# First MLP in blocks: six buffers for y on its way out, the next group's x fetched as soon as blocks are made, own banks for the last chunk's y, another lag count for VectorE

## The chip, the cores and the metric

One core of one Trainium2 chip. The metric is the device time of one execution in microseconds (us). Of the kernel before there are three timed runs, 1055.63, 1056.96 and 1057.51 us (median 1056.96), and one profiled execution of 1056.06 us whose span in the trace is 1054.2 us.

## The reference

Everything is float32. Attention with random features feeds a two-layer MLP, and that a gated one:

```python
def phi(x):                      # x scaled by D**-0.25, omega is 128 x 64
    h = x @ omega.T - (x * x).sum(-1, keepdims=True) / 2
    return exp(h - h.max(-1, keepdims=True)) / sqrt(128)
num, den = phi(q) @ (phi(k).T @ v), phi(q) @ phi(k).sum(seq) + 1e-6
x = (num / den) rearranged from (4, 8, 576, 64) to (2304, 512)
h = x @ w_in                                                  # 512 -> 2048
y = (maximum(h, 0) + alpha * minimum(h, 0)) @ w_out           # 2048 -> 512
out = ((y @ w_a) * (y @ w_b)) @ w_out2                        # 512 -> 1536 -> 512
```

## The kernel before

**Products.** Each float32 operand is split into a high part and a low part, and a product is three matmuls (high by high, high by low, low by high). ScalarE makes a high part by a copy (`xh`, `gh`, `w`), VectorE the low part by a subtraction (`xl`, `gl`, `w` again).

**Weights** lie in DRAM as raw bits. A decoder (`D_`) loads a raw tile, has ScalarE make `z` and `r` from it and VectorE run a chain `z`, `a`, a custom instruction on `a`, and the low half of `w`; some pieces are stored (`store`) and fetched again later (`w<-store`). `D_.pace()` runs the next decode steps as long as `behind()`, the modelled lag of VectorE behind TensorE, is small. That model is `dve_cost` (L181): per instruction a fixed 0.15 and so many columns per us. `hilo(q)` asks for weight q and first runs all the decoding that is still missing up to it, at once.

**Stages.** Times are of the span. To 264.8 us: attention, and beside it the first 4 of 16 feature blocks of the first MLP in 9 chunks of 256 rows (class `Mlp`: `front` makes h, prelu and the split, `back` multiplies by the output weights and sums y in PSUM; `yo` is y on its way to DRAM, `ypart`). From 264.8 to 599.9 us: the other 12 feature blocks in nine groups, n = 0 to 8, each a third of the features (`ps`) by a third of the rows (`tp`), in the order (0,0), (0,1), (0,2), (1,2), (1,1), (1,0), (2,0), (2,1), (2,2). From 599.9 us: the gated MLP in nine groups of the same kind.

**A group of the first MLP** has a `gate_dual` (L1183), seven products of block sums of x and of weights (`GATE_NAMES`: A11, A12, S1, S2, S4, S3, A22) for two halves m, and a `gate_back` (L1227), eight output tiles of 12 matmuls. A product leaves PSUM by ScalarE (`s_g`, `e_g`, `u_g`) or is added on VectorE. Products accumulate in banks named by chain, W, E and B. S2, S3 and A22 are each added onto what stands in the bank of chain W, so each starts only when ScalarE has copied out the one before (`s_g`, then `u_g` twice). An output tile leaves through `leave` (L1252): ScalarE copies it to `yp`, one of three buffers of the tag "op" in pool `io`, and GpSimd's queue sends it with an add to `ypart`.

**x of the next group.** If the next group has other rows, a generator `gens(n)` (L1270) loads them (`load_x`, tile `xg`, from `xpart`) at the group's start, lets one step pass and then runs `combine`, which forms the sums on VectorE (`sumS1g`, ...) and splits each block (`xhg..`, `xlg..`). `tick` takes one step of the generator at every second half-product; what is emitted is what stands in each engine's queue, in that order. Groups 0, 1, 3, 4, 6 and 7 are followed by other rows; group 8 prepares the gated MLP's first rows from `ypart`; groups 2 and 5 prepare nothing.

**The gated MLP.** Per group two `dual` calls (j = 0, 1) and a `back` (L1080), output `o`. The output weights of groups 0, 3 and 6 are decoded as they are first needed.

**Queues.** All loads, and the stores of weights, are issued in order from one queue, SP's (`load_dma`); `ypart<-yp` from GpSimd's (POOL).

Of the kernel before, what the change touches and what calls it, by code (L numbers as in the profile page):

```python
# [9 lines left out]
F32 = mybir.dt.float32  # L10
F32R = mybir.dt.float32r
U32 = mybir.dt.uint32
AF = mybir.ActivationFunctionType
# [5 lines left out]
P = 128  # L19
# [3 lines left out]
DM = 512  # L23
# [11 lines left out]
CI = 256  # L35
# [4 lines left out]
TN = 384  # L40
# [17 lines left out]
def tile_kernel(ctx: ExitStack, tc: tile.TileContext, qT, kT, v1, omT, wbits, alpha, out):  # L58
# [21 lines left out]
    def t_(pool, tag, name, cols=TN, dt=F32, bufs=None):  # L80
        return pool.tile([P, cols], dt, tag=tag, name=name, bufs=bufs)
# [73 lines left out]
        load["dve"] += 0.1 + cols_of(out) / 960  # L155
        vector.tensor_tensor(out=out, in0=in0, in1=in1, op=op)

    clock = {"pe": 0.0, "dve": 0.0, "dma": 0.0}

    def size_of(ap):  # L160
        return math.prod(ap.shape[1:])
# [19 lines left out]
    def dve_cost(name, *a, out=None, in_=None, **k):  # L181
        out = a[0] if out is None else out
        n = size_of(in_ if name == "tensor_reduce" else out)
        clock["dve"] = max(clock["dve"], clock["pe"]) + (0.15 + n / 1890 if name == "tensor_scalar" else 0.15 + n / 960)

    def load_dma(out, in_):
        n = size_of(out) * 4 * P if out.shape[0] == P else 0
# [265 lines left out]
    class Mlp:  # L453
# [7 lines left out]
        def tile(self, kind, name, dt=F32R):  # L461
            n = self.n[kind] = self.n.get(kind, -1) + 1
            m, i, c = n // 4 % 2, n // 2 % 2, n % 2
            if kind in ("xh", "xl"):
                return t_(gp, f"g{kind[1]}{m}{i}{c}", name, dt=dt)[:, :CI]
            if kind == "u":
                return t_(tpb, f"u3{c}", name, dt=dt)[:, :CI]
            return t_(tpa, ("s1" if kind == "gh" else "e5") + "001"[n % 3], name, dt=dt, bufs=(2, 2, 1)[n % 3])[:, :CI]

        def banks(self, psh, tag):  # L470
            self.psy = st_p.enter_context(tc.tile_pool(name="psy", bufs=2, space=PSUM))
# [16 lines left out]
        def front(self, o, n, f, last):  # L488
            hilo(2 * f + 1)
            passed(24 * n / 2400)  # L490
            load["act"] += n / 1000
            load["dve"] += 1.2 * n / 1000
            wh, wl = hilo(2 * f)
            hp = self.psh.tile([P, 512], F32, tag=self.htag, name=f"h{o}_{f}")[:, :n]
            parts = [[(wh, 0)], [(wl, 0)], [(wh, 1)]] if f == 0 else [[(wh, 0)], [(wh, 1)], [(wl, 0)]]
            i = 0
            for part in parts:
                for k in range(KT):
                    ks = slice(k * P, (k + 1) * P)
                    for w_, low in part:  # L500
                        tensor.matmul(hp, lhsT=w_[:, ks], rhs=self.xs[o, k][low],
                                      start=(i == 0), stop=(i == 3 * KT - 1))
                        i += 1
                if D_.free_run:
                    D_.pace(PACE, 1)
            D_.free[2 * f] = last
            u_ = self.tile("u", f"u{o}_{f}", F32)
            nc.scalar.activation(u_, hp, AF.Relu, scale=-1.0)
            vector.scalar_tensor_tensor(out=hp, in0=u_, scalar=bend[:, f:f + 1], in1=hp,
                                        op0=ALU.mult, op1=ALU.add)  # L510
            gh = self.tile("gh", f"gh{o}_{f}")
            gl = self.tile("gl", f"gl{o}_{f}")
            load["act"] += n / 1000
            load["dve"] += 1.3 * n / 1000

            def low():
                vector.tensor_tensor(out=gl, in0=hp, in1=gh.bitcast(F32), op=ALU.subtract)

            def high():
                nc.scalar.activation(gh, hp, AF.Copy)  # L520

            self.gs[o, f] = (gh, gl)
            self.beside(high, low)
            self.q.append((o, n, f, last))

        def back(self, o, n, f, end):
            first, last = f == 0, f == NF0 - 1
            if first:
                ts = [self.psy.tile([P, 2, 256], F32, tag="y", name=f"y{o}_{e}") for e in range(2)]
                self.ys[o] = [ts[e // 2][:, e % 2, :n] for e in range(KT)]  # L530
            ys = self.ys[o]
            wh, wl = hilo(2 * f + 1)
            gh, gl = self.gs.pop((o, f))
            for e in range(KT):
                es = slice(e * P, (e + 1) * P)
                for i, (w_, r_) in enumerate(((wh, gh), (wh, gl), (wl, gh))):
                    tensor.matmul(ys[e], lhsT=w_[:, es], rhs=r_,
                                  start=(first and i == 0 and e % 2 == 0), stop=(last and i == 2 and e % 2 == 1))
                if D_.free_run and e % 2:
                    D_.pace(PACE, 1)  # L540
            D_.free[2 * f + 1] = end
            if last:
                for e in range(KT):
                    if e % 2 == 0:
                        yo = io.tile([P, DM], F32, tag="op", name=f"yo{o}_{e}", bufs=3).rearrange("p (e n) -> p e n", e=2)
                        nc.scalar.activation(yo[:, 0], ys[e], AF.Copy)
                    else:
                        vector.tensor_copy(yo[:, 1], ys[e])
                        nc.sync.dma_start(out=ypart[:, e - 1:e + 1, o:o + n], in_=yo)
                self.ys.pop(o)  # L550

# [440 lines left out]
        return h[:, 256 * i:256 * i + 256], l[:, 256 * i:256 * i + 256]  # L992

    later = []

    def drain(n=1):
        for _ in range(n):
# [11 lines left out]
    def dual(ps, tp, j, last, gen=None, g0=0):  # L1009
        nm_ = f"{ps}{tp}{j}"  # L1010
        banks, sb = [{}, {}], [{}, {}]

        def keep(m, nm, bufs):
            sb[m][nm] = t_(tpb if nm in ("u3", "w7") else tpa, f"{nm}{m}", f"{nm}{m}_{nm_}", bufs=bufs)
            return sb[m][nm]

        for p, nm in enumerate(A_NAMES):
# [18 lines left out]
            E = [e if e is None else e[:, :TN] for e in E]  # L1036
            if nm == "A11":
                for m in range(2):
                    act(keep(m, "s1", 2 - m), W[m])
            elif nm == "S1":  # L1040
                for m in range(2):
                    act(keep(m, "e5", 2 - m), E[m])
            elif nm == "S2":
                for m in range(2):
                    act(keep(m, "u2", 2 - m), W[m])
            elif nm == "S4":
                for m in range(2):
                    vec(sb[m]["u2"], E[m], sb[m]["u2"], ALU.add)
                vec(sb[0]["u2"], sb[0]["u2"], sb[1]["u2"], ALU.mult)
            elif nm == "S3":  # L1050
                for m in range(2):
                    act(keep(m, "u3", 1), W[m])
                split(ps, tp, j, 0, 1, sb[0]["u2"])()
            elif nm == "A12":
                for m in range(2):
                    vec(sb[m]["s1"], banks[m]["B"][:, :TN], sb[m]["s1"], ALU.add)
                vec(sb[0]["s1"], sb[0]["s1"], sb[1]["s1"], ALU.mult)
                if j:
                    low = split(ps, tp, j, 0, 0, sb[0]["s1"])
                else:  # L1060
                    low = lambda: None
                    later.append(lambda: split(ps, tp, j, 0, 0, sb[0]["s1"])())
                for m in range(2):
                    vec(sb[m]["e5"], sb[m]["u3"], sb[m]["e5"], ALU.add)
                low()
            else:
                act(keep(0, "w7", 1), W[0])
                vec(sb[0]["w7"], sb[0]["w7"], W[1], ALU.mult)
                vec(sb[0]["e5"], sb[0]["e5"], sb[1]["e5"], ALU.mult)
                later.append(lambda: split(ps, tp, j, 1, 1, sb[0]["e5"])())  # L1070
                later.append(lambda: split(ps, tp, j, 1, 0, sb[0]["w7"])())
# [66 lines left out]
                    next(gen, None)  # L1138
                D_.pace(PACE, 1)

    agenda, now = [], [0]

    def soon(n, fn):
        agenda.append((now[0] + n, fn))
# [39 lines left out]
    def gate_dual(ps, tp, last, gen):  # L1184
# [1 line left out]
        banks, sb = [{}, {}], [{}, {}]  # L1186

        def keep(m, nm):
            sb[m][nm] = t_(tpb if nm == "u3" else tpa, f"{nm}{m}", f"{nm}{m}_g{ps}{tp}",
                           bufs=1 if nm == "u3" else 2 - m)  # L1190
            return sb[m][nm]

        for p, nm in enumerate(GATE_NAMES):
# [39 lines left out]
    def gate_back(ps, tp, last, gen):  # L1233
        q = Q0 + QA * ps + 7
        for i in range(2):
            for e in range(KT):
# [13 lines left out]

                def leave(ob=ob, e=e, i=i):
                    o = tp * 2 * TN + i * TN  # L1252
                    op = io.tile([P, DM], F32, tag="op", name=f"yp{ps}_{o}_{e}", bufs=3)[:, :TN]
                    act(op, ob)
                    nc.gpsimd.dma_start(out=ypart[:, e, o:o + TN], in_=op, accum_op=ALU.add)  # L1255

# [10 lines left out]
    last_of = lambda n: n % NTP == NTP - 1  # L1267
    follow = lambda n: seq[n + 1] if n + 1 < len(seq) and seq[n + 1][1] != seq[n][1] else None

    def gens(n):  # L1270
        if n == 0:
            yield from first_x
            yield
        if n + 1 == len(seq):
            load_x(ypart, 0)
            yield from combine(A_NAMES, "00")
        elif follow(n):
            load_x(xpart, follow(n)[1])
            yield
            yield from combine(GATE_NAMES, "g%d%d" % follow(n))  # L1280

    for n, (ps, tp) in enumerate(seq):
        gen = gens(n)
        gate_dual(ps, tp, last_of(n), gen)
        gate_back(ps, tp, last_of(n), gen)
        for _ in gen:
            pass
    tick()
    while agenda:
        tick()  # L1290
# [72 lines left out]
```

## Time and profile before

| | |
|---|---|
| timed runs, median (lowest to highest) | 1056.96 us (1055.63 to 1057.51) |
| profiled execution, its own time | 1056.06 us |
| its span in the trace | 1054.2 us |
| mean granted TensorE clock | 0.961 of full |
| TensorE (PE) busy | 960.1 us, 91% |
| VectorE (DVE) busy | 700.1 us, 66% |
| ScalarE (ACT) busy | 595.5 us, 56% |
| GpSimd (POOL) busy | 238.8 us, 23% |
| moved by DMA | 159.96 MB, 152 GB/s on average |

The engines run beside each other, each through its own queue in order. So TensorE's idle time, and the time it runs at a lower granted clock, is what a change to the other engines can give back; an engine's idle time that TensorE doesn't wait for costs nothing. Rows of the trace give start and length in us and, in square brackets, how long the engine was idle just before and what released it.

### The profile page before, as it was taken

Reading aid. Unit: us, or ns where it says so; the run is one execution under the profiler, and the core shown is the slowest. Engines: PE = TensorE matmul, PEld = TensorE weight load, DVE = VectorE, ACT = ScalarE, POOL = GpSimd, SP = SyncE. Lnnn points to the kernel's source line nnn. Section 1 sums busy time; section 2 is a strip of 40 time slices with the busy share of each in tenths; the row PEclk is TensorE's granted clock in tenths of the full one; section 3 lists DMA queues with packets and bytes.
Section 4 is the critical chain, followed back from the end, with each engine's and each line's share of the span. In section 5 each row is a group of like instructions: output and inputs, shape, how many; then the busy total and the mean of one; then the engine's idle time right before and its main releaser. Section 6 shows DMA issues by size and latency. Waiting matters only on the chain.

```text
span 1054.2 us, 17763 instructions
## 1 busy us (share of the span) xinstructions
PE 960.1 (91%) x6663; PEld 895.6 (85%) x6663; DVE 700.1 (66%) x1460; ACT 595.5 (56%) x1440; POOL 238.8 (23%) x226
## 2 busy tenths in 40 slices
PE   8999999987898979898978997999969999959998
PEld 7788898876898979898977995989968999949997
DVE  5887887965756546864595476677574866583633
ACT  6866777753555645665474555565555565544541
POOL 4666556670022102111201200000001010001000
PEclk9999999998899989999999998999989999989999
DMA  8634675567664885397616622335415278405232
GB/s 292 225 122 165 218 275 198 180 230 282 228 138 70 239 253 109 77 241 193 163 20 158 159 81 70 130 136 204 180 39 123 78 161 256 83 21 120 32 59 60
DMA packets 64853, 159.96 MB, mean 152 GB/s; under 512 B 6144, under 2 KB 28032, under 8 KB 64768
## 3 DMA queue, kind: packets, MB, share of 16 engines
q1 hardware_dynamic: 49504, 135.90, 36.7%
q0 software_dynamic: 15120, 22.81, 15.9%
q8 instruction: 52, 0.85, 0.3%
q14 instruction: 33, 0.27, 0.1%
q10 hardware_dynamic: 144, 0.13, 0.0%
HBM read 96.43 MB, written 62.39 MB: 151 GB/s over the span
## 4 chain that ended last, share of the span: by engine, by line
PE 56%; DVE 17%; ACT 11%; DMA 9%; issue 4%; POOL 2%; SPq 0%; ACTq 0%; DVEq 0%; POOLq 0%
PE o L173 13%; PE W L173 12%; PE y L173 11%; PE E L173 6%; DVE a L173 4%; DMA ypart<-yp 3%; DMA xg<-xpart 3%; ACT ph L655 3%; PE B L173 3%; PE W_g L173 3%; PE h L173 2%; DVE xl L483 2%; DVE u_g L173 1%; POOL ypart L1255 1%; DVE w L173 1%
## 5 line engine op out<-in xcount | busy, mean ns | idle before, releaser
L173 PE MATMUL o<-w,gh 128*128 128x512 f32 x432 | 141.1, 407 | 29.3 <-ACT w L148 28.6
L1255 POOL DMA_DIRECT2D ypart<-yp x72 | 63.0, 874 | 304.1 <-ACT yp L148 154.2
L173 PEld LDWEIGHTS o<-w,gh 128*128 128x128 f32 x432 | 84.4, 196 | 51.3 <-ACT w L148 30.9
L1119 POOL DMA_DIRECT2D out<-op x30 | 26.2, 872 | 405.1 <-ACT xh11S L148 195.7
L173 PE MATMUL o<-w,gl 128*128 128x512 f32 x216 | 86.6, 401 | 0.0
L148 ACT ACTIVATE yp<-y 128x384 f32<-128x384 f32 x72 | 35.2, 488 | 79.5 <-DMA ypart<-yp 54.7
L173 PE MATMUL y<-gh,w 128*128 128x256 f32 x288 | 61.9, 298 | 8.5 <-DVE yo L173 8.5
L148 ACT ACTIVATE op<-o 128x512 f32<-128x512 f32 x51 | 30.5, 598 | 59.0 <-PE o L173 43.9
L148 ACT ACTIVATE u<-W 128x384 f32<-128x384 f32 x72 | 35.0, 493 | 46.4 <-PE W L173 45.8
L173 DVE TENSOR_SCALAR z<-z 128x512 uint32<-128x512 uint32 x41 | 17.3, 423 | 60.0 <-ACT z L235 59.8
L173 PEld LDWEIGHTS y<-gh,w 128*128 128x128 f32 x288 | 49.0, 198 | 8.9 <-DVE yo L173 8.9
L173 DVE CUSTOM_DVE_ANT_0 a<-a,r 128x1024 uint16<-128x1024 uint16 x68 | 49.2, 723 | 5.9 <-ACT u L148 0.5
L173 PE MATMUL h<-xh,w 128*128 128x256 f32 x288 | 50.0, 300 | 3.2 <-ACT xh L480 1.3
L173 PEld LDWEIGHTS o<-w,gl 128*128 128x128 f32 x216 | 42.3, 196 | 8.8
L237 POOL TENSOR_SCALAR z<-raw 128x512 f32<-128x512 f32 x28 | 44.2, 1579 | 17.1 <-DMA raw<-in_w 17.0
L240 ACT ACTIVATE r<-raw 128x512 uint32<-128x512 uint32 x68 | 46.3, 683 | 0.8 <-DMA raw<-in_w 0.8
L173 PEld LDWEIGHTS h<-xh,w 128*128 128x128 f32 x288 | 40.6, 198 | 5.2 <-ACT xh L480 1.7
L244 POOL TENSOR_SCALAR a<-raw 128x512 f32<-128x512 f32 x27 | 42.5, 1575 | 0.0
L173 PE MATMUL y<-gl,w 128*128 128x256 f32 x144 | 41.8, 290 | 0.0
L173 DVE TENSOR_TENSOR w<-a,w 128x512 fp32r<-128x512 f32 (+1 forms) x27 | 17.0, 630 | 29.4 <-ACT w L148 29.4
L520 ACT ACTIVATE gh<-h 128x256 fp32r<-128x256 f32 x36 | 13.9, 385 | 38.8 <-DVE h L173 38.8
L173 DVE TENSOR_TENSOR u<-E,u 128x384 f32<-128x384 f32 x36 | 19.1, 553 | 20.5 <-PE E L173 18.8
(1270 smaller groups left out, 3128.9 us busy)
## 6 DMA issues: line engine op xcount, KB each, us to landing
raw<-in_w SPq DMA_DIRECT2D x68, 512.0 KB, 5.5
w<-store SPq DMA_DIRECT2D x47, 512.0 KB, 5.4
store<-t_None SPq DMA_DIRECT2D x41, 512.0 KB, 3.0
ypart<-yp POOLq DMA_DIRECT2D x72, 192.0 KB, 4.7
xg<-ypart SPq DMA_DIRECT2D x14, 768.0 KB, 7.0
xg<-xpart SPq DMA_DIRECT2D x12, 768.0 KB, 9.9
out<-op POOLq DMA_DIRECT2D x30, 256.0 KB, 5.0
q<-in_qT SPq DMA_DIRECT2D x8, 576.0 KB, 4.9
```

The lines of the kernel that those rows point to most:

```text
L148: nc.scalar.activation(out, in_, AF.Copy)
L173: return call(*a, **k)
L237: nc.gpsimd.tensor_scalar(out=z.bitcast(F32), in0=high, scalar1=2.0 ** -112, scalar2=None, op0=ALU.mult)
L240: nc.scalar.activation(r, self.raw[i][:, :, 0], AF.Copy, scale=2.0 ** -29)
L244: nc.gpsimd.tensor_scalar(out=sg.bitcast(F32), in0=high, scalar1=0.0, scalar2=None, op0=ALU.mult)
L483: nc.vector.tensor_tensor(out=lo, in0=src, in1=hi.bitcast(F32), op=ALU.subtract)
L520: nc.scalar.activation(gh, hp, AF.Copy)
L655: nc.scalar.activation(ph[:, 2 * pr + j], pair[j][:, o + pr], AF.Exp, bias=nm[:, j, o + pr:o + pr + 1])
L1119: nc.gpsimd.dma_start(out=dst, in_=op, accum_op=ALU.add)
L1255: nc.gpsimd.dma_start(out=ypart[:, e, o:o + TN], in_=op, accum_op=ALU.add)
```

## The change

- **Buffers.** The tiles that hold a product on its way (`s1`, `e5`, `u2`, and `gh`, `gl` of class `Mlp`) take nine named slots a0 to a8 of pool `tpa`. The groups of the first MLP use six of them, so `yp` alternates between the three buffers of "op" and the free slots a1, a4 and a7.
- **x.** `load_x` of the next other rows is issued as soon as `combine` has formed the blocks of the ones before. The list `todo` keeps what is next, and `combine` starts one step into a group (three in group 0, behind the rest of the x blocks begun in the last chunk).
- **Last chunk.** Its y lies in PSUM banks of the pool behind `bank()`, not in the two of `psy`. Neither `front` nor `back` runs `D_.pace` in it.
- **yo.** Once attention is over, ScalarE copies both halves of `yo`; before, VectorE copied the second.
- **Lag count.** `tensor_scalar` counts 0.12 less in the model. The fixed part is 0.15 for the others up to the end of the first MLP and 0.08 for all from the gated MLP on.

```diff
-    clock = {"pe": 0.0, "dve": 0.0, "dma": 0.0}
+    clock = {"pe": 0.0, "dve": 0.0, "dma": 0.0, "op": 0.15}
...
-        clock["dve"] = max(clock["dve"], clock["pe"]) + (0.15 + n / 1890 if name == "tensor_scalar" else 0.15 + n / 960)
+        clock["dve"] = max(clock["dve"], clock["pe"]) + (0.03 + n / 1890 if name == "tensor_scalar" else n / 960) + clock["op"]
...
-            return t_(tpa, ("s1" if kind == "gh" else "e5") + "001"[n % 3], name, dt=dt, bufs=(2, 2, 1)[n % 3])[:, :CI]
+            return t_(tpa, f"a{n % 3 + 3 * (kind == 'gl')}", name, dt=dt)[:, :CI]
...
-                if D_.free_run:
+                if D_.free_run and not last:
                     D_.pace(PACE, 1)
...
-                ts = [self.psy.tile([P, 2, 256], F32, tag="y", name=f"y{o}_{e}") for e in range(2)]
+                ts = [bank(f"y{o}_{e}").rearrange("p (e n) -> p e n", e=2) if end
+                      else self.psy.tile([P, 2, 256], F32, tag="y", name=f"y{o}_{e}") for e in range(2)]
...
-                if D_.free_run and e % 2:
+                if D_.free_run and e % 2 and not end:
                     D_.pace(PACE, 1)
...
-                        vector.tensor_copy(yo[:, 1], ys[e])
+                        if D_.free_run:
+                            nc.scalar.activation(yo[:, 1], ys[e], AF.Copy)
+                        else:
+                            vector.tensor_copy(yo[:, 1], ys[e])
...
         def keep(m, nm):
-            sb[m][nm] = t_(tpb if nm == "u3" else tpa, f"{nm}{m}", f"{nm}{m}_g{ps}{tp}",
-                           bufs=1 if nm == "u3" else 2 - m)
+            tag = f"u3{m}" if nm == "u3" else "a%d" % ({"s1": 0, "e5": 3, "u2": 6}[nm] + 2 * m)
+            sb[m][nm] = t_(tpb if nm == "u3" else tpa, tag, f"{nm}{m}_g{ps}{tp}")
...
                 def leave(ob=ob, e=e, i=i):
                     o = tp * 2 * TN + i * TN
-                    op = io.tile([P, DM], F32, tag="op", name=f"yp{ps}_{o}_{e}", bufs=3)[:, :TN]
+                    n = n_yp[0] = (n_yp[0] + 1) % 6
+                    nm = f"yp{ps}_{o}_{e}"
+                    op = (t_(tpa, f"a{(1, 4, 7)[n // 2]}", nm) if n % 2 else
+                          io.tile([P, DM], F32, tag="op", name=nm, bufs=3)[:, :TN])
...
+    todo = [(xpart, follow(n)[1], GATE_NAMES, n) for n in range(len(seq)) if follow(n)]
+    todo.append((ypart, 0, A_NAMES, len(seq) - 1))
+
     def gens(n):
         if n == 0:
             yield from first_x
-            yield
-        if n + 1 == len(seq):
-            load_x(ypart, 0)
-            yield from combine(A_NAMES, "00")
-        elif follow(n):
-            load_x(xpart, follow(n)[1])
-            yield
-            yield from combine(GATE_NAMES, "g%d%d" % follow(n))
+            load_x(*todo[0][:2])
+        if todo and todo[0][3] == n:
+            _, tp, names, _ = todo.pop(0)
+            for _ in range(1 if n else 3):
+                yield
+            yield from combine(names, f"{n}_{tp}")
+            if todo:
+                load_x(*todo[0][:2])
...
+    clock["op"] = 0.08
     tick()
```

Three places show how instructions move. ScalarE in group 0 of the first MLP, around the last copies of chain W (`u_g`: those of S2 come first, those of S3 behind them) and the first high parts of the next x (`xhg01A`, after the change `xh_1A`), before:

```order
L1165 ACTIVATE u00001g<-u_g_4509 128x384
L1165 ACTIVATE u00101g<-u_g_4521 128x384
L148 ACTIVATE xhg01A_4543<-xg 128x384
L148 ACTIVATE xhg01A_4545<-xg 128x384
L148 ACTIVATE u_g_4553<-W_g_4429 128x384
L148 ACTIVATE gh00001g<-u_g_4509 128x384
L1165 ACTIVATE u00011g<-e_g_4482 128x384
L148 ACTIVATE u_g_4568<-W_g_4441 128x384
L148 ACTIVATE gh00101g<-u_g_4521 128x384
L1165 ACTIVATE u00111g<-e_g_4495 128x384
```

and with the change:

```order
L148 ACTIVATE u_g_4527<-W_g_4444 128x384
L1175 ACTIVATE u00001g<-u_g_4514 128x384
L1175 ACTIVATE u00101g<-u_g_4527 128x384
L148 ACTIVATE u_g_4560<-W_g_4429 128x384
L148 ACTIVATE gh00001g<-u_g_4514 128x384
L1175 ACTIVATE u00011g<-e_g_4487 128x384
L148 ACTIVATE u_g_4575<-W_g_4444 128x384
L148 ACTIVATE gh00101g<-u_g_4527 128x384
L1175 ACTIVATE u00111g<-e_g_4501 128x384
L148 ACTIVATE xh_1A_4585<-xg 128x384
L148 ACTIVATE xh_1A_4587<-xg 128x384
```

Before, two high parts of the next x stand ahead of both copies of S3; with the change they stand behind them.

SP's queue over groups 0 and 1, where each load of x (`xg<-xpart`) is two transfers, before:

```order
L189 DMA xg<-xpart 128x2x768 x2
L189 DMA store_134<-t_None 128x1024
L189 DMA store_135<-t_1_4512 256x1x256
L189 DMA raw_4822<-in_w 128x1024
L189 DMA xg<-xpart 128x2x768 x2
L189 DMA store_136<-t_None 128x1024
L189 DMA raw_5195<-in_w 128x1024
L189 DMA w_103<-store_126 128x1024
L189 DMA store_137<-t_None 128x1024
L189 DMA w_104<-store_127 128x1024
L189 DMA raw_5302<-in_w 128x1024
```

and with the change:

```order
L189 DMA store_134<-t_None 128x1024
L189 DMA xg<-xpart 128x2x768 x2
L189 DMA store_135<-t_1_4441 256x1x256
L189 DMA raw_4529<-in_w 128x1024
L189 DMA xg<-xpart 128x2x768 x2
L189 DMA store_136<-t_None 128x1024
L189 DMA raw_4898<-in_w 128x1024
L189 DMA xg<-xpart 128x2x768 x2
L189 DMA store_137<-t_None 128x1024
L189 DMA w_103<-store_126 128x1024
L189 DMA raw_5277<-in_w 128x1024
L189 DMA w_104<-store_127 128x1024
```

The load for group 2 keeps its place in the queue; that for group 4 stands behind it by three rows, where it stood 19 rows further on.

VectorE at the end of the second `dual` of group 3 of the gated MLP: the end of the last decodes of output weights (w_4067, w_4068, w_4069, w_95), before:

```order
L173 TENSOR_TENSOR w_4067<-a_9462,w_4067 128x512
L173 TENSOR_SCALAR z_9569<-z_9569 128x512
L173 SCALAR_TENSOR_TENSOR a_9575<-raw_9282,z_9569 128x512
L173 ISA a_9575<-a_9575,r_9571 128x1024
L173 TENSOR_TENSOR w_4068<-a_9575,w_4068 128x512
L173 TENSOR_TENSOR gl_9588<-e_121_9422,gh_9587 128x384
L173 TENSOR_TENSOR gl_9599<-w_121_9550,gh_9598 128x384
L173 TENSOR_SCALAR z_9609<-z_9609 128x512
L173 SCALAR_TENSOR_TENSOR a_9615<-raw_9460,z_9609 128x512
L173 ISA a_9615<-a_9615,r_9611 128x1024
L173 TENSOR_TENSOR w_4069<-a_9615,w_4069 128x512
L173 TENSOR_SCALAR z_9621<-z_9621 128x512
```

and with the change:

```order
L173 TENSOR_TENSOR w_4068<-a_9468,w_4068 128x512
L173 TENSOR_TENSOR gl_9596<-e_121_9442,gh_9595 128x384
L173 TENSOR_TENSOR gl_9607<-w_121_9571,gh_9606 128x384
L173 TENSOR_SCALAR z_9617<-z_9617 128x512
L173 SCALAR_TENSOR_TENSOR a_9623<-raw_9370,z_9617 128x512
L173 ISA a_9623<-a_9623,r_9619 128x1024
L173 TENSOR_TENSOR w_4069<-a_9623,w_4069 128x512
L173 TENSOR_SCALAR z_9629<-z_9629 128x512
L173 SCALAR_TENSOR_TENSOR a_9635<-raw_9466,z_9629 128x512
L173 ISA a_9635<-a_9635,r_9631 128x1024
L173 TENSOR_TENSOR w_95<-a_9635,w_95 128x512
```

Before, a whole decode (`z`, `a`, ISA, `w`) stands ahead of the two `gl` and two more behind (of the last, only `z` is shown); with the change there are two in all, both behind them.

## Rows read from the trace of the kernel before

**Rows 1.** The page: busy time of the engines, and TensorE's granted clock in 40 slices.

```profile
PE 960.1 (91%) x6663; PEld 895.6 (85%) x6663; DVE 700.1 (66%) x1460; ACT 595.5 (56%) x1440; POOL 238.8 (23%) x226
...
PEclk9999999998899989999999998999989999989999
```

**Rows 2.** Waits of TensorE, longest groups: us in total, times, longest.

```profile
PE W_g L173 <- ACT u_g L148: 31.6, 18, 5.9
PE o L173 <- ACT w L148: 28.6, 4, 9.3
```

**Rows 3.** Windows, groups 0 to 8: us, busy PE PEld DVE ACT POOL, PEclk, DMA share, GB/s.

```profile
264.83:302.67 37.84, 34.22 (x182) 33.90 (x181) 25.41 (x53) 22.02 (x51) 6.26 (x7) 0.91 0.68 196
302.67:340.77 38.10, 33.96 (x181) 32.35 (x181) 24.53 (x50) 22.48 (x51) 6.91 (x8) 0.96 0.49 90
340.77:372.97 32.20, 31.78 (x181) 31.14 (x181) 17.55 (x32) 18.41 (x39) 6.17 (x8) 1.00 0.89 231
372.97:414.79 41.82, 33.85 (x182) 32.57 (x182) 27.30 (x55) 21.57 (x49) 5.77 (x7) 0.92 0.61 181
414.79:449.75 34.96, 32.24 (x182) 31.04 (x182) 22.66 (x46) 21.11 (x49) 7.56 (x10) 1.00 0.51 94
449.75:481.45 31.70, 31.47 (x181) 31.15 (x181) 19.66 (x37) 19.63 (x42) 8.51 (x10) 1.00 0.89 219
481.45:521.06 39.61, 33.71 (x182) 32.42 (x181) 23.89 (x48) 21.13 (x48) 5.22 (x6) 0.96 0.66 175
521.06:560.49 39.43, 34.16 (x181) 32.52 (x181) 25.20 (x52) 20.93 (x48) 6.79 (x8) 0.96 0.46 99
560.49:599.92 39.43, 34.87 (x181) 33.40 (x181) 23.17 (x47) 22.00 (x51) 8.46 (x11) 0.91 0.56 120
```

**Rows 4.** Timeline of TensorE: waits of 0.4 us and more in groups 3 and 4.

```profile
389.47 0.69 PE L173 MATMUL W_g<-xhg02S,w 128*128 128x384 f32 x1 [5.93 <-ACT u_g L148]
...
428.84 0.45 PE L173 MATMUL W_g<-xhg11A,w 128*128 128x384 f32 x1 [1.20 <-ACT u_g L148]
...
431.64 0.44 PE L173 MATMUL W_g<-xhg11A,w 128*128 128x384 f32 x1 [1.48 <-ACT u_g L148]
```

**Rows 5.** Timeline of ScalarE ahead of TensorE's wait in group 3.

```profile
386.56 0.52 ACT L148 ACTIVATE xhg11A<-xg 128x384 fp32r<-128x384 f32 x1 [5.96 <-DMA xg<-xpart]
...
388.94 0.47 ACT L148 ACTIVATE u_g<-W_g 128x384 f32<-128x384 f32 x1
```

**Rows 6.** Waits of ScalarE for a buffer of y.

```profile
ACT yp L148 <- DMA ypart<-yp: 54.7, 27, 5.0
```

**Rows 7.** DMA issues: count, size, median us from issue to landing.

```profile
ypart<-yp POOLq DMA_DIRECT2D x72, 192.0 KB, 4.7
...
xg<-xpart SPq DMA_DIRECT2D x12, 768.0 KB, 9.9
```

**Rows 8.** Last chunk: timelines of TensorE and VectorE.

```profile
255.84 0.58 PE L173 MATMUL y<-gh,w 128*128 128x256 f32 x1 [6.17 <-DVE yo L173]
...
253.15 1.03 DVE L173 TENSOR_TENSOR sumS1g<-xg 128x384 f32<-128x384 f32 x2 [6.43 <-issue]
```

**Rows 9.** Gated MLP, group 3: TensorE's wait, then VectorE's ends of the forced decodes.

```profile
789.23 1.52 PE L173 MATMUL o<-w,gh 128*128 128x512 f32 x2 [9.30 <-ACT w L148]
...
793.43 0.69 DVE L173 TENSOR_TENSOR w<-a,w 128x512 fp32r<-128x512 f32 x1 [0.70 <-ACT w L148]
...
796.71 0.69 DVE L173 TENSOR_TENSOR w<-a,w 128x512 fp32r<-128x512 f32 x1 [0.70 <-ACT w L148]
```

**Rows 10.** Windows of the gated MLP, group 3: both duals, and the 29.24 us behind them.

```profile
750.60:779.76 29.16, 29.16 (x169) 28.99 (x167) 21.13 (x42) 17.64 (x37) 0.00 (x0) 1.00 0.40 144
779.76:809.00 29.24, 19.71 (x71) 15.04 (x71) 20.42 (x40) 14.38 (x29) 3.45 (x4) 0.77 0.33 64
```

**Rows 11.** The page, costliest groups: y's issue by GpSimd and copy by ScalarE.

```profile
L1255 POOL DMA_DIRECT2D ypart<-yp x72 | 63.0, 874 | 304.1 <-ACT yp L148 154.2
...
L148 ACT ACTIVATE yp<-y 128x384 f32<-128x384 f32 x72 | 35.2, 488 | 79.5 <-DMA ypart<-yp 54.7
```

## What was predicted before the changed kernel ran

> **What bounds the kernel now.** I read the page first: TensorE is busy for 960.1 us of a span of 1054.2, so about 94 us are idle, and its clock is granted in full except in a few slices [rows 1]. Every engine has slack on average (VectorE is busy for 700.1 us), so what counts is where TensorE stops. Its waits say so [rows 2]: 31.6 us on `u_g` and 28.6 us on `w` ahead of the gated MLP's output. With one wait in the last chunk these make three places.
>
> *Groups of the first MLP.* The windows [rows 3] show nine pieces with the same number of matmuls, 181 or 182, in 31.70 to 41.82 us. The two short ones that prepare no x (32.20 and 31.70) are nearly all TensorE work: 31.47 busy in 31.70. Of the seven others only group 4 is short, 34.96 us. The clock column belongs to it: 1.00 in the short ones, 0.91 or 0.92 in groups 0, 3 and 8. Half-clock time follows the longer waits, so a wait removed returns more than itself.
>
> In group 3 TensorE waits 5.93 us for `u_g` [rows 4]. ScalarE shows why [rows 5]: high parts of the next x stand in its queue ahead of that copy, and the first waits 5.96 us for the transfer `xg<-xpart`; `u_g` itself, at 388.94, waits for nothing else. Such a load takes 9.9 us from issue to landing (median), twice the time of the others [rows 7]. I read the same in groups 0 and 6. In groups 1, 7 and 8 the cause sits in the group before: ScalarE waits 54.7 us in 27 waits for a `yp` buffer [rows 6], and VectorE's and ScalarE's work for the following products queues behind it. Group 4, whose x came early enough, keeps two small waits, 1.20 and 1.48 us [rows 4]: there the order of sums, splits and copies on two engines is what remains.
>
> *Start of `back` in groups 0, 3 and 6 of the gated MLP.* In group 3 TensorE waits 9.30 us for `w`, and the decodes that were left to the end follow at a distance of 3.28 us, 793.43 to 796.71 [rows 9]. The 29.24 us behind the two duals hold only 71 matmuls, at a clock of 0.77 [rows 10].
>
> *Last chunk.* TensorE waits 6.17 us at 255.84 for a `yo` copy that stands behind `sumS1g`, which starts at 253.15 after 6.43 us of idling [rows 8].
>
> **The change, part by part.** The sum is made against the profiled execution, 1056.06 us; the median of the runs is 0.9 us higher, less than the 0.2% (2.1 us) that a measurement of this kernel can tell from no change.
>
> *x fetched earlier.* In SP's queue the loads for groups 4 and 7, whose blocks groups 3 and 6 make, move up by 16 and 12 places, past raw tiles, stores and weights that now follow them; the other four stay within a place. In group 0 the high parts of the next x move behind both copies of S3. I price a group whose x is there in time by group 4, the one that shows it [rows 3]: 37.84 - 34.96 = 2.9 us in group 0, 41.82 - 34.96 = 6.9 in group 3, 39.61 - 34.96 = 4.7 in group 6, together 14.4. In group 0 the splits are also out of the way of S3, so about half of group 4's two waits, 1.5 us, goes too. The transfers themselves aren't shorter; those for groups 4 and 7 now have about a group's length, over 30 us, to land. What SP's queue holds behind them waits until `combine` has read the old x; the cover is that raw tiles are loaded three ahead, and it costs nothing while that lasts.
>
> *Six buffers.* An output tile is 12 of a group's 180 matmuls, so 31.70 x 12 / 180 = 2.1 us. Three buffers come round in 6.3 us. A buffer is taken for the copy (0.49), the issue (0.87) [rows 11] and the landing (4.7 [rows 7]), 6.1 us: half of the tiles wait, which is what 27 waits of 72 [rows 6] say. Six come round in 12.6 us, and landings up to 11 us are covered. So I take groups 1, 7 and 8 to group 4's length too [rows 3]: 3.1 + 4.5 + 4.5 = 12.1 us. *Against this stands* the Trainium skill, "DMA: Bandwidth & Descriptors", section "Anatomy of one DMA — SWDGE (gpsimd) path", whose fit of 2.0 us plus bytes by 436 GB/s gives an estimate of 2.45 us for 192 KB; three buffers would then suffice and the six be worth nothing. The trace shows 4.7 us, so I go by the row.
>
> All gate groups: 14.4 + 1.5 + 12.1 = 28.0. Bounds from the rows: all nine at 31.70 would give 335.09 - 285.3 = 50 us (335.09 is the sum of [rows 3]); if only late x goes, 14.4.
>
> *Last chunk.* Its own banks take away the 6.17 us wait on `yo`. But the same VectorE queue holds the `gl` of the next blocks, and it still stands at `sumS1g` until 253.15 [rows 8], since that transfer of x isn't moved. And the first matmuls of group 0 now reuse banks that ScalarE must empty of `yo` first, where they waited for nothing. Four short copies move from VectorE to ScalarE, where slack is larger [rows 1]. What is late next is `gl`. Between -6.2 and +3 us (a wait on ScalarE of the size that TensorE had in group 4, 1.20 + 1.48) I take 0, as the cause of the lateness stays.
>
> *Lag count.* It moves decoding only. With about 40 VectorE instructions in two duals, 0.07 less for each makes the model some 3 us less behind, so roughly one decode (3.28 us [rows 9]) comes earlier. In group 3 one of three decodes at the end moves into the duals, where VectorE works for 21.13 of 29.16 us [rows 10], so 8 us are free there: 3.3 us saved. In group 6 one decode and one low half (0.69): 4.0. In group 0 only one low half moves: 0.7. Together 8.0, and 1 us for less time at half clock. Bounds: 0, and the whole 28.6 us of [rows 2].
>
> **Sum:** 1056.06 - 28.0 - 0 - 9.0 = 1019 us. Its own range is 1008 to 1030, with the gate groups half way to 50 us or as far short.
>
> **The rivals.**
>
> *A. The buffers aren't what holds groups 1, 7 and 8.* The wait on `yp` would move to the transfer: `yp` and the earlier x loads share the 16 DMA engines, busy for 0.89 in groups 2 and 5 [rows 3], and with landings over 11 us six buffers fill as three did, or these groups are held by the order of sums and splits that remains in group 4. Then 12.1 us stay: 1019 + 12 = 1031. For it: x loads take 9.9 us [rows 7]. Against: the DMA share is 0.46 to 0.56 in groups 1, 7 and 8. By the Trainium skill's fit above, too, the buffers would be worth nothing and the time this one.
>
> *B. The start of `back` doesn't shorten.* The decode done in the duals pushes the `gl` that `back` also needs, or the forced ones now wait for raw tiles: 1019 + 9 = 1028. Against: 8 us of free VectorE time [rows 10].
>
> *C. Slower: decoding moved into the duals stands ahead of what TensorE needs.* VectorE works in order, and a decode of 3.28 us ahead of an addition or a `gl` in each of 18 duals would make TensorE wait, in duals that today run without any wait (29.16 busy in 29.16 [rows 10]). All of it lost: 18 x 3.28 = 59 us, so 1019 + 9 + 59 = 1087. It passes the gain of the gate groups from 28/18 = 1.6 us for each dual on. Against: the slack between a product and the next on its chain is a product of 12 matmuls, 2.1 us, and in most groups no decoding is left over.
>
> *D. No change.* If the loads were held by the DMA engines and not by their place in the queue (share 0.89 in groups 2 and 5 [rows 3]), they would land as late, and the `yp` with them: 1056, within 2.
>
> **How the numbers follow.** Forecast 0.58, A 0.20, B 0.10, C 0.06, D 0.06. The predicted time is 1019. The range takes the forecast's own, A and B, and reaches down to 1003, as the gate groups' upper bound is 22 us further, and up to 1038, where A and B come together with a last chunk that loses: it holds 0.83. Faster by over 0.2%: forecast, A, B and a part of D, 0.90; same 0.04 (most of D); slower 0.06 (C).
>
> **What would show it.** Right: groups 0, 1, 3, 6, 7 and 8 at 34 to 36 us; no wait of ScalarE on `xg<-xpart` ahead of a `u_g`; `yp` waits below 10 us in all; no wait at 255.84; `o` waits in groups 3 and 6 of the gated MLP shorter by 3 to 4 us, that in group 0 nearly as long as before; a TensorE wait near 258 us on `gl`. A: groups 1, 7, 8 still at 38 to 39 us with `yp` waits on the transfer. B: three `o` waits of about 9 us. C: waits inside duals. The prediction is wrong if a wait that isn't in these rows takes more than 15 us, or if group 4's two waits turn out to be another thing than the order of the queues.

## The result, and the profile after

The changed kernel takes 1018.94 us (median of 4 runs, 1017.25 to 1022.83), the kernel before 1057.24 on the same chips: a ratio of 0.9646, interval 0.9614 to 0.9677. The profiled execution took 1020.14 us, its span is 1018.4, 35.8 less than before. One execution of the first experiment's kernel took 5130.11 us, its 128x512 matmuls 1.69 us instead of 0.40 at a granted clock of 1.00 in the records; its time is left out of that kernel's, though the profile is of it. The page after, beside [rows 1]:

```profile
PE 949.8 (93%) x6663; PEld 889.2 (87%) x6663; DVE 698.1 (69%) x1456; ACT 595.8 (59%) x1444; POOL 238.8 (23%) x226
...
PEclk8999999999899999999999999999989999979999
```

VectorE and ScalarE do the same work as before; TensorE's busy time falls by 10.3 us, as less of it runs at half clock (the mean granted clock is 0.972, before 0.961), and its idle time by 25.5. The waits of TensorE, beside [rows 2] (us in total, times, longest):

```profile
PE o L173 <- ACT w L148: 17.9, 4, 7.8
PE W_g L173 <- ACT u_g L148: 14.7, 15, 1.5
PE o L173 <- DVE w L173: 5.9, 3, 5.5
```

Waits for `u_g` are halved, and none is longer than 1.5 us where the longest was 5.9. ScalarE has no wait for a buffer of y left, 54.7 us before [rows 6], and waits once, 0.8 us, for a transfer of x from `xpart`. The groups 0 to 8 of the first MLP, in the columns of [rows 3]:

```profile
267.03:298.87 31.84, 31.60 (x181) 31.29 (x181) 25.61 (x52) 22.44 (x52) 6.26 (x7) 1.00 0.71 190
298.87:335.31 36.44, 33.47 (x181) 32.65 (x181) 24.23 (x48) 21.74 (x49) 5.49 (x7) 0.95 0.57 147
335.31:367.03 31.72, 31.51 (x182) 31.19 (x181) 18.11 (x33) 19.41 (x41) 8.47 (x10) 1.00 0.95 261
367.03:401.73 34.70, 32.09 (x182) 31.13 (x181) 26.37 (x54) 21.53 (x49) 5.23 (x6) 1.00 0.60 162
401.73:435.45 33.72, 32.04 (x181) 31.08 (x181) 23.26 (x47) 21.42 (x49) 6.98 (x8) 1.00 0.54 124
435.45:467.63 32.18, 31.75 (x181) 31.11 (x181) 18.35 (x35) 18.32 (x39) 8.74 (x10) 1.00 0.95 249
467.63:503.15 35.52, 33.21 (x182) 32.58 (x181) 24.59 (x50) 22.57 (x51) 5.22 (x6) 0.95 0.60 155
503.15:537.73 34.58, 32.03 (x182) 31.07 (x182) 25.52 (x52) 20.95 (x48) 6.98 (x8) 1.00 0.45 95
537.73:571.61 33.88, 32.04 (x182) 31.08 (x182) 22.53 (x46) 20.91 (x48) 7.83 (x9) 1.00 0.69 156
```

Their sum is 304.58 us instead of 335.09, so 30.5 us of the 35.8 lie here. The clock column is at 1.00 in seven of nine groups, before in three. In the gated MLP groups 0, 3 and 6 are 0.8, 4.3 and 2.5 us shorter (columns as above):

```profile
571.61:630.55 58.94, 48.18 (x241) 43.42 (x241) 41.70 (x80) 31.61 (x66) 1.75 (x2) 0.94 0.36 113
721.65:776.31 54.66, 47.96 (x242) 43.72 (x240) 40.32 (x78) 31.04 (x64) 3.60 (x5) 0.94 0.39 110
867.32:923.52 56.20, 48.45 (x241) 44.22 (x240) 36.92 (x70) 29.05 (x62) 5.22 (x7) 0.91 0.30 66
```

The last chunk gives 0.7 us. Against that attention took 2.9 us more in this execution. Five kernels below have the same code as the changed one up to there, and their first groups start between 264.26 and 267.21 us (267.03 here), so this is a difference between executions.

### The profile page after: what moved, and what is told of

It reads as the page before. It is cut to its first block, busy times and chain, and to the rows that moved or that the text cites. A ratio compares the mean times of both kernels' runs of the same rounds, so it can differ in the third digit from the quotient of the medians.

```text
span 1018.4 us, 17782 instructions
## 1 busy us (share of the span) xinstructions
PE 949.8 (93%) x6663; PEld 889.2 (87%) x6663; DVE 698.1 (69%) x1456; ACT 595.8 (59%) x1444; POOL 238.8 (23%) x226
## 4 chain that ended last, share of the span: by engine, by line
PE 67%; DVE 17%; ACT 8%; DMA 4%; issue 3%; POOL 1%; SPq 0%; DVEq 0%; ACTq 0%; POOLq 0%
PE y L173 17%; PE o L173 14%; PE W L173 14%; PE E L173 7%; PE W_g L173 3%; DVE a L173 3%; PE B L173 3%; ACT ph L659 2%; PE h L173 2%; DVE sumS L173 1%; DVE xl L483 1%; DMA w<-store 1%; DVE u_g L173 1%; PE E_g L173 1%; PE B_g L173 1%
## 5 line engine op out<-in xcount | busy, mean ns | idle before, releaser
L173 PE MATMUL y<-gh,w 128*128 128x256 f32 x288 | 64.1, 305 | 4.6 <-ACT gh L520 2.5
L173 PE MATMUL kv<-v,ph 128*64 128x65 f32 x640 | 29.3, 235 | 6.0 <-ACT ph L659 5.4
```

What stands on the lines that cost most here:

```text
L173: return call(*a, **k)
```

## The experiments

### The parts taken out of the changed kernel, one at a time

**Three buffers for y.**

```diff
-                    op = (t_(tpa, f"a{(1, 4, 7)[n // 2]}", nm) if n % 2 else
-                          io.tile([P, DM], F32, tag="op", name=nm, bufs=3)[:, :TN])
+                    op = io.tile([P, DM], F32, tag="op", name=nm, bufs=3)[:, :TN]
```

> The changed kernel with y leaving through the three buffers of the tag op alone; all else as changed. My theory (the buffers are what holds groups 1, 7 and 8): 12 us of the gain go, about 1031 us, ScalarE's waits for ypart<-yp return to 50 us or more, and groups 1, 7 and 8 are 38 to 39 us long. Rival A (buffers are idle; x order did it): within 2 us of the changed kernel, about 1019 us.

Measured: 1037.01 us (1035.05 to 1041.13), ratio to the kernel before 0.9809 (0.9775 to 0.9843). The buffers are worth 18 us here, more than the 12 priced. No profile shows in which groups.

**The old fetch of x.** `gens` as before (in the diff ahead of the prediction, the lines with a minus).

> The changed kernel with x loaded and its blocks made at the places of the kernel before (load at the group's start, blocks one step on, two in group 0). My theory (late x holds groups 0, 3 and 6): 14 to 16 us of the gain go, about 1034 us, with xhg.. waiting for xg<-xpart in groups 0, 3 and 6 and those groups at 38 to 42 us, groups 1, 7 and 8 still near 35. Rival (the buffers alone did it, since loads were late only because y's transfers stood in their way): about 1019 us.

Measured: 1040.23 us, 0.9828 (0.9804 to 0.9852), 21 us lost. Groups 3 and 6 are 41.2 and 42.0 us long, with waits for `u_g` of 5.85 and 6.67 us. Group 0 is 35.4, group 1 34.4, group 7 34.6. Group 8, which the prediction gave to the buffers, is 40.6 with all six of them: its x, from `ypart`, is loaded at 550.63, just after the group starts, where the changed kernel loads it at 530.36, 7.4 us ahead of it. Late x does hold groups 3 and 6, and group 8 too.

**The old lag count.** `dve_cost` as before.

> The changed kernel with the old count of VectorE's lag (0.15 for every instruction, all through). My theory (the count moves decodes ahead in the gated MLP): 7 to 8 us go, about 1026 us. Rival (the order of decodes in group 3 moved because x is fetched earlier, as the rows of this kernel's VectorE queue show two decodes behind the last gl there as in the changed one, and three only in group 6): 2 to 4 us go, about 1022 us, all of it in group 6.

Measured: 1026.0 us, 0.9699 (0.9679 to 0.9719): 7 us lost. Groups 3 and 6 of the gated MLP are back at 58.62 and 58.64 us, so the count did it in both; the early fetch without the new count leaves both at 58.6 us too (the run with the fetch alone, below).

**The old last chunk.** `psy`, VectorE's half of `yo` and `pace` as before.

> The changed kernel with the last chunk as before: y in the two banks of psy, the second half of yo copied by VectorE, pace run in it. My theory (VectorE stands at sumS1g all the same): within 2 us of the changed kernel, about 1019 us, with a wait for yo of 4 to 6 us at the last chunk's first y in place of shorter ones behind it. Rival (the wait for yo was what the chunk lost): 4 to 6 us go, about 1024 us.

Measured: 1015.49 us, 0.9593 (0.9569 to 0.9616), 3.4 us less than the changed kernel. The wait for `yo` is back at 6.13 us, and the chunk is 1.5 us longer (35.07 against 33.55 us); the saving lies in the groups, 301.5 us instead of 304.6. Neither expectation holds. Two of these 3 us come with no edit at all: the run with the lag count at 0 (below) has the changed kernel's code in these groups, and its groups 1 and 6 take 35.39 and 34.38 us at a granted clock of 1.00, where the changed kernel's took 36.44 and 35.52 at 0.95, with the same longest waits (1.5 us). A later pair comes back to it.

### The parts put into the kernel before, alone

**Six buffers and the slots.**

> The kernel before with the six buffers for y (and the slots a0 to a8) alone: old fetch of x, old lag count, old last chunk. Prediction's pricing: groups 1, 7 and 8 fall to 35 us, 12 us gained, about 1045 us, no waits of ScalarE for ypart<-yp, groups 0, 3 and 6 still at 38 to 42 us. Rival (buffers and fetch only work together, since each wait hides behind the other): under 5 us gained, 1053 us or more.

Measured: 1044.28 us, 0.9887 (0.9872 to 0.9902), 12 us gained as priced. Groups 1 and 7 fall to 34.4 and 33.8 us, group 8 only to 37.6. Groups 3 and 6 stay at 41.83 and 40.46. The slots a0 to a8, part of this run and of the next, were not run by themselves.

**The early fetch and the slots.**

> The kernel before with the early fetch of x (and the slots a0 to a8) alone: three buffers for y, old lag count, old last chunk. Prediction's pricing: groups 0, 3 and 6 fall to 35 us, 14 to 16 us gained, about 1042 us, waits for ypart<-yp still near 55 us. Rival (what the three-buffer run lost, 20 us, was the buffers' due only because early x keeps the DMA engines busy in the backs): waits for ypart<-yp over 60 us and about 10 us gained, 1048 us.

Measured: 1037.94 us, 0.983 (0.9803 to 0.9857), 18 us gained (the three-buffer run lost 18 us, not the 20 of the expectation). ScalarE's waits, this kernel:

```profile
ACT yp L148 <- DMA ypart<-yp: 65.8, 33, 3.7
```

The waits for buffers are longer than before, 65.8 us against 54.7 [rows 6], and yet groups 1 and 8, which the prediction put down to them, fall to 35.3 and 35.0 us. Group 7 pays most, with 41.30 us. Groups 2 and 5, which make no blocks, pay too: 34.99 and 33.55 us, where they took 32.20 and 31.70 [rows 3]. ScalarE's queue at the start of group 7 shows how:

```profile
502.36 0.49 ACT L148 ACTIVATE yp<-y 128x384 f32<-128x384 f32 x1 [3.58 <-DMA ypart<-yp]
506.41 0.49 ACT L148 ACTIVATE yp<-y 128x384 f32<-128x384 f32 x1 [3.56 <-DMA ypart<-yp]
508.50 0.49 ACT L148 ACTIVATE yp<-y 128x384 f32<-128x384 f32 x1 [1.60 <-DMA ypart<-yp]
510.86 0.49 ACT L148 ACTIVATE yp<-y 128x384 f32<-128x384 f32 x1 [1.87 <-DMA ypart<-yp]
...
512.35 0.85 ACT L148 ACTIVATE s_g<-W_g 128x384 f32<-128x384 f32 x2
```

The group's TensorE work starts at 503.83, and A11's copies `s_g` leave only at 512.35, behind the last group's four `yp`. Chain W waits 2.64 us there. In group 2 it is the same, with a wait of 1.55 us. So a wait for a buffer counts when it reaches into the next group's chain, not by its own length.

### The place of the blocks

What was left in the changed kernel, 0.4 to 1.5 us before S3 and A22 in every group that makes blocks but group 0, pointed to another common cause. In group 3 of the changed kernel, ScalarE:

```profile
378.56 0.53 ACT L1175 ACTIVATE u12001g<-u_g 128x384 f32<-128x384 f32 x1 [1.50 <-DVE u_g L173]
379.03 0.53 ACT L1175 ACTIVATE u12101g<-u_g 128x384 f32<-128x384 f32 x1
379.46 0.92 ACT L148 ACTIVATE xh_1S<-sumS 128x384 fp32r<-128x384 f32 x2
380.29 0.47 ACT L148 ACTIVATE u_g<-W_g 128x384 f32<-128x384 f32 x1
```

and VectorE at the same time:

```profile
376.10 1.02 DVE L173 TENSOR_TENSOR xl_1A<-xg,xh_1A 128x384 fp32r<-128x384 f32 x2
377.04 1.02 DVE L173 TENSOR_TENSOR sumS<-xg 128x384 f32<-128x384 f32 x2
377.98 1.02 DVE L173 TENSOR_TENSOR u_g<-E_g,u_g 128x384 f32<-128x384 f32 x2
```

Nothing waits for a transfer any more. Low parts and sums of the next x stand ahead of the addition for S4, ScalarE waits 1.50 us for that, and the copy of S3 comes at 380.29, behind two splits. These blocks are needed only a group later.

**Blocks later.** In the changed kernel:

```diff
-            for _ in range(1 if n else 3):
+            for _ in range(4 if n else 3):
```

> The changed kernel with combine starting four steps into groups 1, 3, 4, 6, 7 and 8 instead of one, so that the splits of the next x stand behind both copies of S3 in ScalarE's queue, as in group 0. My theory (what is left of the waits for u_g in these groups, 0.4 to 1.5 us each, comes from sums and splits ahead of S3): these waits vanish, each group falls by 2 to 3 us to about 32, 12 to 16 us gained on the changed kernel, about 1005 us. Rival (the work only moves, and the first product of the next group or the back waits instead): within 3 us of the changed kernel.

Measured: 997.31 us, 0.9446 (0.9432 to 0.946): 21.6 us gained on the changed kernel, more than expected. All nine groups are 31.7 to 32.2 us long, TensorE waits for no `u_g` for 0.4 us or more, and the first two duals of the gated MLP gain 2.9 us. Groups 1, 3 and 6, in the columns of [rows 3]:

```profile
296.09:327.80 31.71, 31.50 (x181) 31.18 (x181) 25.19 (x49) 22.10 (x50) 6.96 (x8) 1.00 0.61 133
359.51:391.56 32.05, 31.70 (x182) 31.14 (x182) 26.65 (x54) 21.82 (x49) 6.96 (x8) 1.00 0.65 150
455.45:487.67 32.22, 31.80 (x182) 31.15 (x182) 26.10 (x52) 22.42 (x51) 6.54 (x8) 1.00 0.64 138
```

The loads of x keep their places in SP's queue, so here it is the place of the blocks alone that counts.

**Blocks later in the kernel before**, with nothing else of the change:

```diff
             load_x(xpart, follow(n)[1])
-            yield
+            for _ in range(4):
+                yield
```

> The kernel before with one edit: combine starts four steps after the load of x in groups 0, 1, 3, 4, 6 and 7, the load staying at the group's start. Theory (late x costs only because its splits stand ahead of copies that TensorE needs): 18 to 25 us gained by this edit alone, 1033 to 1038 us, no wait of TensorE for u_g behind a wait for xg<-xpart. Rival (x must also be there earlier, or y's three buffers hold the groups): under 10 us gained, 1047 us or more.

Measured: 1017.12 us, 0.9628 (0.9611 to 0.9645): this edit alone gives as much as the whole change, and more than expected. Three of its groups (3, 7 and 8), in the columns of [rows 3]:

```profile
361.39:393.20 31.81, 31.50 (x182) 31.18 (x182) 26.66 (x54) 22.20 (x50) 7.13 (x9) 1.00 0.82 216
...
489.38:521.09 31.71, 31.47 (x182) 31.15 (x181) 25.49 (x52) 21.95 (x50) 7.42 (x9) 1.00 0.58 121
521.09:563.34 42.25, 34.82 (x182) 33.54 (x182) 22.43 (x46) 20.15 (x46) 6.27 (x8) 0.92 0.58 161
```

Groups 0 to 7 take 31.7 to 32.3 us with x loaded at the old place and three buffers. In group 3 x is still late: its two transfers land 13.7 and 15.6 us into the group, before 13.6 and 15.5. ScalarE's last copy of S3 and the first split of the next x:

```profile
374.86 0.47 ACT L148 ACTIVATE u_g<-W_g 128x384 f32<-128x384 f32 x1
...
376.54 1.03 ACT L148 ACTIVATE xhg11A<-xg 128x384 fp32r<-128x384 f32 x2
```

The split runs 15.2 us into the group; before, it ran 13.6 us into it [rows 5]. It comes at nearly the same time, but now behind the copy and not ahead of it. Group 8, whose blocks the edit left at the group's start, takes 42.25 and serves for comparison in the same run, though its blocks are those for the gated MLP. There VectorE shows the old pattern, a sum 3.98 us late for its transfer and the prelu of the current group behind it:

```profile
531.38 0.56 DVE L173 TENSOR_TENSOR sumS<-xg 128x384 f32<-128x384 f32 x1 [3.98 <-DMA xg<-ypart]
531.85 0.61 DVE L173 SCALAR_TENSOR_TENSOR s_g<-u22100g,bend,s_g 128x384 f32<-128x384 f32 x1
```

ScalarE's waits for `ypart<-yp` in this kernel are 21.5 us in 14, and groups 0 to 7 lose nothing by them.

### More decoding inside the duals

```diff
-    clock["op"] = 0.08
+    clock["op"] = 0.0
```

> The changed kernel with the fixed part of the lag count at 0 instead of 0.08 from the gated MLP on; no decode then stands behind the last gl of groups 3 and 6, while group 0 stays as it is. My theory (a decode put into the duals is hidden there): the waits for w in groups 3 and 6 go, up to 18 us gained on the changed kernel, 1001 to 1006 us, duals still 29.15 us. Rival C (decodes ahead of what TensorE needs slow the duals): duals of groups 2 to 6 of 31 us and more, 1019 us or slower.

Measured: 997.26 us, 0.9445 (0.9429 to 0.9461), 21.7 us gained, more than the 18 expected. Groups 3 and 6 of the gated MLP gain 9.2 and 10.7 us. The whole of group 3 of the gated MLP:

```profile
717.65:763.16 45.51, 45.51 (x242) 42.66 (x240) 37.24 (x74) 29.48 (x62) 3.48 (x4) 1.00 0.48 134
```

TensorE is busy without a gap, with VectorE at 37.24 of 45.51 us. The duals of groups 1 to 8 are still 29.15 us long, so rival C's slower duals don't appear: the decoding moved here is hidden.

### All together

**Late blocks and lag count 0.**

> The changed kernel with blocks made four steps into a group and the lag count at 0 in the gated MLP, together. My theory (the two act in different stages, so their gains add): 1019 - 21.6 - 21.7 = 976 us, groups of the first MLP at 31.7, of the gated MLP at 45.5 but for group 0. Rival (decoding that no longer fits beside the blocks comes back as a wait): 980 us or more.

Measured: 978.91 us, 0.926 (0.9239 to 0.9281). The gains add to within 4 us. What TensorE still waits for, for 1 us or more, behind attention is group 0 of the gated MLP (3.62, 1.74 and 1.27 us for `w`) and the last chunk.

**The same with the old last chunk.**

> The same with the last chunk as before (psy's two banks, the second half of yo by VectorE, pace). If the last chunk's part of the change costs time by itself, as the run with the old last chunk said (1015.5 against 1018.9), 3 us less than with the changed one, about 973 us. If that difference lay in how groups 1 and 6 happened to wait, these waits are gone here and both take the same within 1.5 us.

Measured: 977.94 us, 0.9261 (0.9247 to 0.9275), the same. The chunk's part of the change is worth nothing by itself here; the 3.4 us by which it seemed to slow the changed kernel are gone. Two of them were stretches at a lower clock in groups 1 and 6 that another execution of the same code doesn't show; what the rest was stays open.

**The same as the first with three buffers for y.**

> The first kernel of this call (late blocks, lag count 0) with three buffers for y. Theory (a wait for a buffer of y holds the s_g and e_g copies of the next group's first products, late blocks or not): about 60 us of waits for ypart<-yp and 5 to 12 us slower, 981 to 988 us. Rival (six buffers only paid while the splits stood in the way): within 2 us of it.

Measured: 977.51 us, 0.9256 (0.9241 to 0.927), the same. ScalarE waits 24.7 us in 19 for `ypart<-yp`, and groups 7 and 8 take 31.7 us. Once the blocks come late, six buffers give nothing over three.

## Why the prediction was right, and where its reasons were not

**The sum**: 1019 foretold, 1018.94 measured, inside the forecast's own range. That it hits so closely is luck: the groups gave 2.5 us more than booked, the lag count 1.5 less, the last chunk 0.7 more, attention took 2.9 more in the profiled execution, and the four runs lie 5.6 us apart.

**Groups of the first MLP**: 28.0 foretold, 30.5 measured. Group 4's length as the price of a group without late transfers held: groups 1, 3, 6, 7 and 8 came to 33.9 to 36.4 us. Group 0, with its splits behind S3, came to 31.84, 6.0 us shorter instead of 4.4: moving the splits was worth all of group 4's two waits and more, and I had booked half of them. With late blocks group 4 itself takes 31.7 us, so its two waits were the order of the queues, as said.

**Six buffers**, 12.1 us: alone they gave 12. But the step "So I take groups 1, 7 and 8 to group 4's length too" named one holder where there were more. Group 8 was booked at 4.5 us and got 1.8 from the buffers alone; it was held by its late x. The early fetch alone brought groups 1 and 8 to 35 us with the buffer waits at 65.8 us, and with late blocks three buffers serve as well as six. Waits for `yp` cost where they hold the next group's first copies, as in groups 2, 5 and 7 of the early fetch alone. The count of waits was read loosely, too: 27 of 72 is three tiles in eight, not half, and 6.1 us of use in a round of 6.3 leaves none waiting at the median. By the fit in the Trainium skill ("DMA: Bandwidth & Descriptors", "Anatomy of one DMA — SWDGE (gpsimd) path") an estimate of 2.45 us follows for 192 KB, with which no tile would wait. The traces don't agree: the kernels with three buffers have landings of 4.1 to 5.4 us (medians) and 14 to 33 waits. That three do suffice with late blocks has another reason: 19 waits are left, and no group is longer for them.

**x earlier**, 15.9 us: alone it gave 18, and groups 0, 3 and 6 together 18.2. That x was late was right, as [rows 5] read. That the load of group 8's x, from `ypart`, comes earlier too was not in the sum. And an earlier load was not the only remedy: making the blocks four steps later did more, as it took the sums and splits out of the way.

So the shared cause, shown by late blocks in both kernels, is the place of the next x's sums and splits in the queues of VectorE and ScalarE, ahead of copies that TensorE's chain needs. Late transfers and full buffers made it worse. I had seen it in group 4 ("the order of sums, splits and copies on two engines is what remains") and took it for a remainder of 3 us; in the kernel before, the one edit to that order gave back 39 us.

**Lag count**: 9 foretold, 7.5 in the profile, 7 by the run without it. Group 3 gave 4.3 instead of 3.3, the size of group 6 was off (2.5 instead of 4.0). Both are left with two decodes at the end. In group 3, 17 matmuls of `o` run while VectorE does them, and the waits are 5.47, 1.01 and 0.23 us; in group 6 these matmuls run earlier, and TensorE then waits in one piece:

```profile
908.50 1.52 PE L173 MATMUL o<-w,gh 128*128 128x512 f32 x2 [7.75 <-ACT w L148]
```

Group 6 has the lower granted clock, 0.91 against 0.94. The count itself is not quite as the list of the change has it: by the line of the diff, `tensor_scalar` counts a fixed 0.18 up to the end of the first MLP, 0.03 more than before, and 0.11 from the gated MLP on, 0.04 less. The 0.07 less of the prediction holds for the other instructions.

**Last chunk**: 0 foretold, 0.7 in the profile, nothing by the last pair of runs. As said, VectorE still stands at `sumS1g`. But `gh` is late next, not `gl`, since the prelu that it is made from stands behind that sum:

```profile
257.31 0.39 PE L173 MATMUL y<-gh,w 128*128 128x256 f32 x1 [2.02 <-ACT gh L520]
...
255.41 1.03 DVE L173 TENSOR_TENSOR sumS1g<-xg 128x384 f32<-128x384 f32 x2 [5.34 <-issue]
```

TensorE waits 2.02 and 0.49 us for `gh` and 0.88 for `yo` of the new banks, in place of 6.17.

**What stays open**: taking the buffers out of the changed kernel cost 18 us. The fetch alone, 18, and the lag count, 7, would make 1031 without them, 6 us less than measured. The runs of these two kernels lie 6.1 and 7.4 us apart, so a part may be noise.

## What to carry to other kernels

Work for a later stage is best put into an in-order queue behind what the present stage waits for; here where it stood mattered more than when its data came or how many buffers there were. When a wait disappears with either of two changes, look for a third cause that both relieve. Before pricing a wait by its length, look at whose queue it holds up, and whether TensorE waits for that queue.

## What the runs showed of the hardware

Transfers of one size landed after different times (medians from issue to landing): the 192 KB of `ypart<-yp` took 4.7 us before, 6.0 in the changed kernel and 4.1 with late blocks in the kernel before; the 768 KB of `xg<-xpart` 9.9, 9.3 and 8.8.
